# Fourier mixing with a routed expert layer: batch 0's A ahead of the constants in the store queue, selection and expert steps cut into single VectorE pieces, two bits a round for four batches

## The chip, the cores and the metric

The kernel runs on one core of a Trainium2 chip. The metric is the device time of one execution in microseconds; less is better. TensorE (PE), its weight loads (PEld), VectorE (DVE), ScalarE (ACT) and GpSimd (POOL) each take their instructions in order from a queue of their own, and SyncE (SP) issues nearly all transfers, in order too.

## The reference

Per batch (8 batches, 3136 rows, 256 columns) a real Fourier transform over the rows, a complex 256 by 256 product with bias and a soft threshold, the inverse transform, and then an expert layer for the 128 rows with the highest score.

```python
X = np.fft.rfft(x, axis=1)
Yr = Xr @ w_r - Xi @ w_i + b_r
Yi = Xr @ w_i + Xi @ w_r + b_i
Yr = np.sign(Yr) * np.maximum(np.abs(Yr) - lam, 0.0)   # Yi alike
y = np.fft.irfft(Y, n=x.shape[1], axis=1)
...
scores = np.einsum('bsd,d->bs', x, w_gate)             # x is y here
top_idx = np.argpartition(-scores[b], capacity)[:capacity]
h = np.maximum(xe @ w1, 0.0)
out[b, top_idx] = x[b, top_idx] + g[:, None] * (h @ w2)   # g: sigmoid of the score
```

## The kernel before

The 3136 rows are 98 by 32, so a transform is two short ones. The steps of a batch, with their names in the code and in the profile:
- s1, 8 tiles: x (tile `xt`, in the first batch also `cin`) is added and subtracted in halves (`xu`, `xv`, by GpSimd, in batch 0 by VectorE and GpSimd), multiplied by `first` into `s`, evicted by ScalarE into `at` and stored to DRAM as `As`.
- s2, 6 groups: `av` is loaded from `As`, once all 8 tiles of the batch are stored, multiplied by `second` into `px`, and split into a high and a low part (`Xh`, `Xl`).
- spectral, 6 groups: 24 products with `wh` and `wl` into `py`, then bias and threshold into `Y` (two halves: one by VectorE and ScalarE, the other by VectorE, ScalarE and GpSimd).
- s2i, 6 groups: `Y` times `second` into `s`, evicted into `ct`, stored as `Cs`; VectorE takes the scores' parts from the same banks (`junk`, `Csc`).
- s1i, 8 tiles: `cin` is loaded from `Cs` once the batch is stored, added and subtracted (`cu`, `cv`), multiplied into `s`, evicted into `ot` and stored as `out`.
- selection: the threshold of the 128 best rows is found bit by bit. In each round VectorE compares the scores with trial values (`c`), counts (`n`), PE adds the counts over the partitions (`n,tm` into `px`), and VectorE sets the bits (`ok`, `px`, `w`). With three bits a round 7 trial values are counted at once, and there are 12 rounds. Batches are selected in the groups 0-1, 2-3, 4-5, 6 and 7, one after the other. From the threshold come a mask, row numbers (`hot`, `row`) and `idxs`.
- expert layer, 8 times: GpSimd gathers `xe` by `idxs`; PE transposes it, multiplies by `w1s` and, in three products, by `w2h` and `w2l`; GpSimd scatters `ye` into `out`.

No order is written out by hand. While the program is built, a planner keeps an estimate of when each engine and each tile is free (in `Engine.given`, `mm` and `ld`, with `WIRE` as the queue's rate), and at each step takes the candidate with the lowest cost: waiting time plus its distance from its place in the sequence of 48 spectral steps (`F1` and `I1` place s1 and s1i, `LEAD` and `LAG` s2 and s2i). Loads, stores, sums and late steps are "sides": generators that go on when the planner's clock has come to them. The order so found is what each engine's queue holds; nothing is reordered at run time. After the last spectral step (`spec["t"] >= T`) only s1i, selection and experts are left.

The profile's lines for PE are nearly all L272 (`mm`), for VectorE, ScalarE and GpSimd L220 (the recording helper), for SyncE L301 (`ld`), so tiles' names tell the steps apart.

## Time and profile before

| | |
|---|---|
| median of 3 runs | 751.42 us (751.36 to 752.93) |
| the profiled execution | 746.76 us |
| its span, first to last instruction | 745.0 us |
| mean granted TensorE clock | 0.941 of full speed |
| PE busy | 673.3 us (90%) |
| VectorE, ScalarE, GpSimd busy | 407.5, 361.0, 394.8 us |
| bytes moved | 162.54 MB, mean 218 GB/s |

The engines' times overlap and don't add up to the span. A PE that is called busy isn't always at its full rate, since matmuls are pipelined and their ends are modelled; the row of the granted clock says when it ran slower (0.5 is 1.2 GHz, 1.0 is 2.4 GHz). "GB/s" is what all 16 DMA engines moved, "DMA share" how busy they were on average.

### The profile page before, as it was taken

How to read it: one execution, taken by the hardware profiler on the slowest of the kernel's cores; microseconds unless marked ns; L12 is line 12 of the kernel's file. 1: busy time of each engine (PE TensorE's matmuls, PEld its weight loads, DVE VectorE, ACT ScalarE, POOL GpSimd, SP SyncE). 2: the span in 40 equal slices, each digit the busy share in tenths (PEclk: the TensorE clock that was granted, in tenths of full speed). 3: DMA queues.
4: the chain of work that ended last, by engine and by line, in shares of the span. 5: the costliest groups of instructions: out<-in, count | busy, mean ns of one | idle time of the engine just before them, and what ended most of it. 6: DMA issues, size and time to landing. Idle time of an engine off the chain costs nothing.

```text
span 745.0 us, 19254 instructions
## 1 busy us (share of the span) xinstructions
PE 673.3 (90%) x7608; PEld 426.9 (57%) x7608; DVE 407.5 (55%) x1248; ACT 361.0 (48%) x766; POOL 394.8 (53%) x329
## 2 busy tenths in 40 slices
PE   4359999999999999999999999999989798699895
PEld 1127666666655565665555656665656465248784
DVE  6204455445358756453587664645876477546661
ACT  2324656566656655646556556465635234341110
POOL 5363636675776657747675577374540534362211
PEclk9569999999999999999999999999999899579997
DMA  8895878999798869887988798879845843781000
GB/s 249 280 287 186 257 229 254 223 279 303 233 295 266 287 194 273 263 277 234 277 278 286 211 272 276 280 209 279 247 136 130 214 110 114 173 240 59 29 15 22
DMA packets 85110, 162.54 MB, mean 218 GB/s; under 512 B 6334, under 2 KB 58907, under 8 KB 85019
## 3 DMA queue, kind: packets, MB, share of 16 engines
q1 hardware_dynamic: 83962, 159.13, 71.4%
q0 software_dynamic: 1056, 2.17, 0.9%
q8 instruction: 60, 0.98, 0.6%
q14 instruction: 32, 0.25, 0.1%
HBM read 83.23 MB, written 78.12 MB: 217 GB/s over the span
## 4 chain that ended last, share of the span: by engine, by line
PE 54%; DVE 9%; DMA 8%; issue 5%; POOL 2%; ACT 2%; SPq 0%; POOLq 0%; DVEq 0%; ACTq 0%
PE py L272 31%; PE s L272 17%; PE px L272 6%; DMA Cs<-ct 2%; DMA xt<-in_x 1%; DMA cin<-Ct 1%; DMA As<-at 1%; DVE c L220 1%; DVE px L220 1%; DVE hot L220 1%; DVE junk L220 1%; DMA cin<-Cs 1%; DVE n L220 1%; DVE py L220 1%; POOL xv L220 1%
## 5 line engine op out<-in xcount | busy, mean ns | idle before, releaser
L272 PE MATMUL py<-wh,Xh 128*128 128x512 f32 x384 | 170.5, 444 | 3.0 <-DVE YT L220 2.6
L272 PE MATMUL py<-wl,Xh 128*128 128x512 f32 x384 | 152.8, 398 | 0.0
L272 PE MATMUL py<-wh,Xl 128*128 128x512 f32 x384 | 152.7, 398 | 0.0
L220 POOL TENSOR_TENSOR cu<-cin 113x512 f32<-113x512 f32 x64 | 83.6, 1308 | 126.2 <-PE s L272 87.5
L220 DVE TENSOR_TENSOR Xl<-px,Xh 128x512 fp32r<-128x512 f32 x96 | 61.9, 686 | 132.4 <-ACT Xh L220 132.4
L220 POOL TENSOR_TENSOR xu<-xt 113x512 f32<-113x512 f32 x56 | 71.8, 1282 | 89.1 <-PE s L272 88.9
L272 PEld LDWEIGHTS py<-wh,Xh 128*128 128x128 f32 x384 | 73.1, 190 | 78.0 <-issue 53.4
L272 PE MATMUL s<-xu,first 49*64 49x512 f32 (+1 forms) x256 | 84.4, 661 | 22.3 <-ACT at L220 11.4
L220 ACT COPY ot<-s 113x512 f32<-113x512 f32 x128 | 68.7, 592 | 68.4 <-PE s L272 58.3
L220 ACT COPY at<-s 113x512 f32<-113x512 f32 x128 | 68.6, 588 | 58.9 <-PE s L272 43.2
L220 DVE CUSTOM_DVE_ANT_0 junk<-s,wgb 128x256 f32<-128x256 f32 x192 | 80.9, 421 | 26.3 <-ACT ct L220 12.9
L272 PE MATMUL s<-cu,first 49*64 49x512 f32 (+1 forms) x256 | 83.6, 658 | 7.1 <-POOL cu L220 5.7
L220 POOL TENSOR_TENSOR Y<-r,r 128x512 f32<-128x512 f32 x48 | 61.9, 1290 | 41.4 <-ACT r L220 19.3
L272 PEld LDWEIGHTS py<-wl,Xh 128*128 128x128 f32 x384 | 73.4, 191 | 17.1
L220 POOL TENSOR_TENSOR xv<-xt 113x512 f32<-113x512 f32 x60 | 78.2, 1305 | 8.9 <-DVE xt L220 4.7
L272 PE MATMUL s<-xv,first 49*64 49x512 f32 (+1 forms) x256 | 81.5, 662 | 0.2 <-POOL xv L220 0.2
L272 PE MATMUL s<-cv,first 64*64 64x512 f32 (+1 forms) x256 | 81.6, 661 | 0.0
L272 PEld LDWEIGHTS py<-wh,Xl 128*128 128x128 f32 x384 | 73.7, 192 | 9.5
L272 PEld LDWEIGHTS px<-second,av 64*64 64x64 f32 x3072 | 54.9, 138 | 37.4 <-issue 14.5
L220 ACT COPY ct<-s 128x256 f32<-128x256 f32 x192 | 57.6, 387 | 37.7 <-PE s L272 37.2
L220 POOL TENSOR_TENSOR cv<-cin 113x512 f32<-113x512 f32 x59 | 75.8, 1285 | 0.0
L272 PE MATMUL s<-Y,second 32*64 32x256 f32 x1536 | 65.4, 397 | 6.4 <-ACT ot L220 2.9
(128 smaller groups left out, 951.3 us busy)
## 6 DMA issues: line engine op xcount, KB each, us to landing
As<-at SPq DMA_DIRECT2D x64, 392.0 KB
out<-ot SPq DMA_DIRECT2D x64, 392.0 KB
av<-As SPq DMA_DIRECT2D x48, 512.0 KB
Cs<-ct SPq DMA_DIRECT2D x48, 512.0 KB
cin<-Cs SPq DMA_DIRECT2D x64, 384.0 KB
xt<-in_x SPq DMA_DIRECT2D x60, 392.0 KB
cin<-in_x SPq DMA_DIRECT2D x4, 392.0 KB
second<-t_second SPq DMA_DIRECT2D x2, 768.0 KB
```

Of the source, the lines that this page charges most:

```text
L220: return f(*args, **kw)
L272: return nc.tensor.matmul(out, a, b, start=start, stop=stop)
```

## The change

Four things change. First, the order of the first transfers: the loads of the constants become sides that wait until so many stores of batch 0's A have been issued (`behind_a` with the numbers in `CA`), and batch 0's odd tiles of A use the ring `ot`, which is idle then. Second, the VectorE parts of a selection round (`counts`, `digest`) and the steps of the expert layer (`copies`, `halves`, the final sum) are no longer issued together with their PE part: each is a side, issued when the planner finds VectorE free for it, in selection with a further delay (`LOWA`, `DB`). Third, the first two groups, four batches, take two bits a round: 3 trial values and 17 rounds. Fourth, the planner's numbers change, so the order of all engines changes in places.

```diff
-    WIRE = 370e3
+    WIRE = 300e3
...
     class Side:
-        def __init__(self, g):
-            self.g, self.over, self.need = g, False, None
+        def __init__(self, g, low=None):
...
-                    if w is None or w > t:
+                    if w is None or w > t - (s.low() if s.low else 0.0):
                         break
                     s.step()
                     again = True
+                    if s.low:
+                        break
                 if s.over:
                     sides.remove(s)
...
 
+    def behind_a(n):
+        return lambda: free["SP"] if stored.get(("A", 0), 0) + len(fed) >= n else None
+
+    def consts_s():
+        yield "SP", behind_a(CA[0])
+        ld(sec[0].rearrange("p j s -> p (j s)"), t_second[:, :NJ * 64])
+        yield "SP", behind_a(CA[3])
+        ld(tail, t_tail)
+        yield "SP", behind_a(CA[4])
+        ld(wgb, wg.rearrange("(o e) -> o e", o=1).broadcast_to([128, D]))
+        ld(sec[1].rearrange("p j s -> p (j s)"), t_second[:, NJ * 64:])
+
     def consts_w():
...
         ts = []
         for src in (w_r, w_i):
             ts.append(new(pool, [128, 2, D], F32, "r1", 2))
...
     def consts_bias():
+        vec.memset(m2l, -2.0 * LAM)
+        yield "SP", behind_a(CA[2])
         for c, src in enumerate((b_r, b_i)):
             row = src.rearrange("(o e) -> o e", o=1)
             ld(bias[:, c, :], row.broadcast_to([128, D]))
             ld(bias_t[33 * c:33 + 31 * c], row.broadcast_to([33 - 2 * c, D]))
-        vec.memset(m2l, -2.0 * LAM)
         yield "DVE", [bias, bias_t]
...
+        def counts(f, m):
             c = new(pool, [N1, nb, m, N2], BF16, "c_6" if nb == 1 else "c" + tag, 1)
...
+            yield "DVE", []
...
+        def digest(tot, m, i, nxt):
+            yield "DVE", [tot]
...
+            if nxt is None:
+                yield "DVE", []
...
+            m2, i2 = nxt
+            f = f[:, :, :m2]
+            vec.tensor_tensor(out=f, in0=digits[:, 8 * i2:8 * i2 + m2].rearrange("p (o m) -> p o m", o=1).broadcast_to([N1, nb, m2]),
+                              in1=wp.broadcast_to([N1, nb, m2]), op=ALU.bitwise_xor)
+            yield "DVE", []
+            yield from counts(f, m2)
...
+        rounds = [(2 ** (hi - i) - 1, i) for hi, i in zip([32] + cuts, cuts)]
+        side(first_keys(rounds[0][0]), low)
+        for (m, i), nxt in zip(rounds, rounds[1:] + [None]):
+            yield lambda: avail([st["n"]]) if st["n"] is not None else None
+            name = m_name()
+            tot = m_tile([N1, 4, nb, 2 ** bits - 1])
+            mm(tot[:, 0, :, :m], ones, st["n"])
+            st["n"] = None
+            hold(tot, name, side(digest(tot, m, i, nxt), low))
...
+        def copies():
+            yield "DVE", [px]
+            vec.tensor_copy(xT, px)
...
+            def halves(q, ph):
+                yield "ACT", [ph]
+                act.activation(out=hs[q][0], in_=ph, func=AF.Relu)
+                yield "DVE", [ph, hs[q][0]]
+                vec.scalar_tensor_tensor(out=hs[q][1], in0=ph, scalar=0.0, in1=hs[q][0].bitcast(F32), op0=ALU.max, op1=ALU.subtract)
+                st["h", q] = True
...
+            yield "DVE", [py, ga]
+            ye = new(pool, [n, D], F32, "ye", 1)
+            vec.scalar_tensor_tensor(out=ye, in0=py, scalar=ga, in1=xe, op0=ALU.mult, op1=ALU.add)
...
-        t = new(pool, [PT, 4, D], F32, "at", 3)
+        home = "ot" if b == 0 and i % 2 else "at"
+        t = new(pool, [PT, 4, D], F32, home, 3)
         tv = t.rearrange("p (r c) d -> p r (c d)", r=2)
...
+                fed.add((b, g))
...
-    EARLY, AHEAD, SW = 0.3,1.1,0
-    BACK, TAIL = 99,44
-    LAST = 2
-    PF = (0,0.1)
-    BEGIN, RATE, DB = 2.5,1.6,1
+    EARLY, AHEAD, SW = 0,1.1,0.2
+    BACK, TAIL = 99,40
+    LAST = 3
+    PF = (0,0.3)
+    BEGIN, RATE, DB = 2.5,2.2,0.3
+    LOWA = 0.4
     AHEADT, FA, TD = 0.7,2,0.5
     BE, BU, BY = 99, 99, 1.0
-    DG, GAP = 0.5,2
-    STEP, THW, FIL = 5,4,(8,2)
-    END = 0.1
-    GROUPS = ((0, 2), 3), ((2, 4), 3), ((4, 6), 3), ((6, 7), 3), ((7, 8), 3)
-    F1, I1 = [-1, 0, 0, 1, 2, 2, 3, 3],[9, 10, 10, 11, 12, 12, 13, 14]
-    LEAD, LAG = 0.95,2.06
+    DG, GAP = 0.5,0.5
+    STEP, THW, FIL = 5,4,(8,3)
+    END = 0.3
+    GROUPS = ((0, 2), 2), ((2, 4), 2), ((4, 6), 3), ((6, 7), 3), ((7, 8), 3)
+    F1, I1 = [-1, 0, 0, 1, 2, 2, 3, 3],[10, 10, 11, 12, 12, 13, 14, 15]
+    LEAD, LAG = 1.1,2.06
     NQ = 1
+    CA = 1,2,8,9,10,9
...
-        yield from select(bs, bits)
+        yield from select(bs, bits, lambda: 0.0 if spec["t"] >= T and bs.stop == B else LOWA - DB * owner[10 * bs.start - 200].behind())
...
+        side(a_side())
+        side(consts_s())
+        side(consts_w())
         side(consts_bias())
-        ld(sec[0].rearrange("p j s -> p (j s)"), t_second[:, :NJ * 64])
-        side(consts_w())
-        ld(tail, t_tail)
-        ld(wgb, wg.rearrange("(o e) -> o e", o=1).broadcast_to([128, D]))
-        side(a_side())
-        ld(sec[1].rearrange("p j s -> p (j s)"), t_second[:, NJ * 64:])
```

The order of SyncE's queue at the start, behind the table `first` and the first x tiles: `As` is the store of batch 0's A, `bias`, `second`, `r` (the two weights), `tail` and `wgb` are constants. Before:

```order
L301 DMA cin_94<-in_x 98x1024 x2
L301 DMA bias<-in_b_r 128x256
L301 DMA bias_t<-in_b_r 33x256
L301 DMA bias<-in_b_i 128x256
L301 DMA bias_t<-in_b_i 31x256
L301 DMA second_67<-t_second 128x1536
L301 DMA r_118<-in_w_r 128x2x256
L301 DMA r_120<-in_w_i 128x2x256
L301 DMA tail<-t_tail 64x161
L301 DMA wgb<-in_moe_w_gate 128x256
L301 DMA second_68<-t_second 128x1536
L301 DMA As<-at 98x1024
```

and in the changed kernel:

```order
L301 DMA cin_94<-in_x 98x1024 x2
L301 DMA As<-at 98x1024
L301 DMA second_67<-t_second 128x1536
L301 DMA As<-ot 98x1024
L301 DMA r_160<-in_w_r 128x2x256
L301 DMA r_162<-in_w_i 128x2x256
L301 DMA As<-at 98x1024
L301 DMA As<-ot 98x1024
L301 DMA As<-at 98x1024
L301 DMA As<-ot 98x1024
L301 DMA As<-at 98x1024
L301 DMA As<-ot 98x1024
```

The stores stood behind all constants and now stand between them; bias, `tail`, `wgb` and the second half of `second` come after the eighth store.

GpSimd's queue around the first `cin` of batch 6 (`cu` and `cv` are its sums, `Y` the last step of a half of a spectral group of batch 7). Before:

```order
L220 TENSOR_TENSOR Y<-r_7628,r_7532 128x512
L220 TENSOR_TENSOR cu<-cin_93 113x512
L220 TENSOR_TENSOR cv<-cin_93 113x512
L220 TENSOR_TENSOR cu<-cin_93 113x512
L220 TENSOR_TENSOR cv<-cin_93 113x512
L220 TENSOR_TENSOR Y<-r_7783,r_7677 128x512
L220 TENSOR_TENSOR cu<-cin_94 113x512
L220 TENSOR_TENSOR cv<-cin_94 113x512
L220 TENSOR_TENSOR Y<-r_7850,r_7832 128x512
```

and in the changed kernel:

```order
L220 TENSOR_TENSOR Y<-r_7750,r_7646 128x512
L220 TENSOR_TENSOR cu<-cin_93 113x512
L220 TENSOR_TENSOR cv<-cin_93 113x512
L220 TENSOR_TENSOR Y<-r_7855,r_7792 128x512
L220 TENSOR_TENSOR cu<-cin_93 113x512
L220 TENSOR_TENSOR cv<-cin_93 113x512
L220 TENSOR_TENSOR Y<-r_7979,r_7956 128x512
L220 TENSOR_TENSOR cu<-cin_94 113x512
L220 TENSOR_TENSOR cv<-cin_94 113x512
```

Two pairs of sums stood ahead of the second Y here; now one pair does.

PE's queue at the last selection (`row,hot` makes the row numbers of batch 7; `ident,xe` is the transpose of the rows gathered by them, `xT,w1s` an expert's first layer, `w2h` and `w2l` its second). Before:

```order
L272 MATMUL py<-w2h,hh 128x256
L272 MATMUL py<-w2h,hl 128x256
L272 MATMUL py<-w2l,hh 128x256
L272 MATMUL px_9367<-row,hot 128x34 x2
L285 MATMUL py<-ident,xe 128x128 x2
L272 MATMUL py<-xT,w1s 128x128 x16
L272 MATMUL py<-w2h,hh 128x256
```

and in the changed kernel, where 24 products of the second layer follow and then the transpose:

```order
L272 LDWEIGHTS tm
L272 MATMUL px_9432<-cnt,tm 98x1
L272 MATMUL py<-xT,w1s 128x128 x8
L272 MATMUL px_9455<-row,hot 128x34 x2
L272 MATMUL py<-xT,w1s 128x128 x8
L272 MATMUL py<-w2h,hh 128x256
L272 MATMUL py<-w2h,hl 128x256
L272 MATMUL py<-w2l,hh 128x256
```

The last gather had no PE work behind `row,hot`; now half of a first layer and a whole second layer of batch 6's experts stand there.

## Rows read from the trace of the kernel before

**Rows 1.** The page, parts 1 and 2: busy time, granted clock in 40 slices.

```profile
PE 673.3 (90%) x7608; PEld 426.9 (57%) x7608; DVE 407.5 (55%) x1248; ACT 361.0 (48%) x766; POOL 394.8 (53%) x329
...
PEclk9569999999999999999999999999999899579997
```

**Rows 2.** Stretches on all engines: busy us (instructions), clock, DMA share, GB/s.

```profile
0.00:50.00 50.00, 21.76 (x88) 5.96 (x88) 16.31 (x20) 15.18 (x27) 28.87 (x29) 0.79 0.85 270
50.00:56.00 6.00, 4.44 (x129) 3.95 (x129) 1.29 (x2) 1.21 (x3) 0.42 (x4) 0.50 1.01 293
...
238.00:388.00 150.00, 146.68 (x1781) 88.57 (x1774) 87.69 (x272) 85.23 (x182) 96.97 (x79) 1.00 0.86 259
388.00:534.50 146.50, 145.00 (x1783) 87.84 (x1774) 87.68 (x272) 85.00 (x183) 89.87 (x73) 1.00 0.86 257
```

**Rows 3.** Timeline of ScalarE at the start: start us, us, instruction, idle before.

```profile
13.85 1.07 ACT L220 COPY at<-s 113x512 f32<-113x512 f32 x2 [0.63 <-PE s L272]
15.67 1.07 ACT L220 COPY at<-s 113x512 f32<-113x512 f32 x2 [0.75 <-PE s L272]
26.77 1.07 ACT L220 COPY at<-s 113x512 f32<-113x512 f32 x2 [10.03 <-DMA As<-at]
```

**Rows 4.** Timeline of the queue of SyncE, merged: start us, us, issues.

```profile
23.43 12.05 SPq L301 DMA_DIRECT2D As<-at  x4
...
43.28 1.01 SPq L301 DMA_DIRECT2D av<-As  x2
...
93.93 0.94 SPq L301 DMA_DIRECT2D av<-As  x2
```

**Rows 5.** Timeline of PE at the start.

```profile
50.04 1.99 PE L272 MATMUL px<-second,av 64*64 64x64 f32 x64 [6.66 <-DMA av<-As]
53.42 2.57 PE L272 MATMUL px<-second,av 64*64 64x64 f32 x64 [1.40 <-DVE Xl L220]
55.92 0.79 PE L272 MATMUL py<-wh,Xh 128*128 128x512 f32 x1
```

**Rows 6.** The chain that ended last: start us, us, what (one A load).

```profile
298.22 10.19 DMA As<-at
308.49 4.27 DMA av<-As
```

**Rows 7.** Timeline of PE at the first s2 of batch 1.

```profile
101.49 1.16 PE L272 MATMUL px<-second,av 64*64 64x64 f32 x64 [1.12 <-DMA av<-As]
```

**Rows 8.** Groups by shape, whole span: count, busy us, mean ns, idle before.

```profile
L220 DVE TENSOR_TENSOR c<-scores,px 98x448 bf16<-98x448 f32 x30 | 18.6, 621 | 1.0
L220 DVE TENSOR_REDUCE n<-c 98x14 bf16<-98x448 bf16 x30 | 18.6, 620 | 1.0
...
L220 DVE TENSOR_TENSOR c<-scores,px 98x224 bf16<-98x224 f32 x20 | 7.7, 387 | 0.7
...
L272 PE MATMUL px<-n,tm 98*98 98x14 bf16 x30 | 5.1, 172 | 0.6 <-DVE Xl L220 0.2 <-DVE n L220 0.2
```

**Rows 9.** Timeline of PE in batch 7.

```profile
586.81 1.13 PE L272 MATMUL s<-Y,second 32*64 32x256 f32 x4 [2.90 <-ACT ot L220]
```

**Rows 10.** Timeline of ScalarE in batch 7.

```profile
584.90 0.72 ACT L220 ACTIVATE r<-r,m2l 128x512 f32<-128x512 f32 x1 [6.04 <-POOL Y L220]
```

**Rows 11.** Timeline of GpSimd in batch 7.

```profile
578.66 1.30 POOL L220 TENSOR_TENSOR cu<-cin 113x512 f32<-113x512 f32 x1 [9.05 <-DMA cin<-Ct]
...
583.59 1.27 POOL L220 TENSOR_TENSOR Y<-r,r 128x512 f32<-128x512 f32 x1
```

**Rows 12.** Timeline of PE at the end.

```profile
715.80 2.12 PE L272 MATMUL py<-xT,w1s 128*128 128x128 f32 x17
...
722.20 0.36 PE L272 MATMUL py<-w2h,hh 128*128 128x256 f32 x1
...
725.14 0.53 PE L272 MATMUL px<-row,hot 98*128 98x34 f32 x4
...
730.19 0.69 PE L285 MATMUL py<-ident,xe 128*128 128x128 f32 x2 [4.51 <-DMA xe<-out,idxs]
```

More of the change, by code (lines that the diff above doesn't have):

```diff
@@ L347, in fourier_moe @@
     class Side:
-        def __init__(self, g):
-            self.g, self.over, self.need = g, False, None
+        def __init__(self, g, low=None):
+            self.g, self.over, self.need, self.low = g, False, None, low
             self.step()
@@ L363, in fourier_moe, with side @@
     sides = []
-    def side(g):
-        s = Side(g)
+    def side(g, low=None):
+        s = Side(g, low)
         if not s.over:
@@ L497, in m_tile, with select @@
         return new(ps, shape, F32, name, 1)
-    def select(bs, bits):
+    def select(bs, bits, lag):
         nb = bs.stop - bs.start
@@ L506, in select @@
             cuts.append(max(cuts[-1] - bits, 0))
-        w = wp = None
-        for hi, i in zip([32] + cuts, cuts):
-            m = 2 ** (hi - i) - 1
-            if w is None:
-                f = new(pool, [N1, nb, m], U32, "f" + tag, 1)
-                vec.memset(f, 0)
-            else:
-                f = small[:, 3, :, :m]
-                vec.tensor_tensor(out=f, in0=digits[:, 8 * i:8 * i + m].rearrange("p (o m) -> p o m", o=1).broadcast_to([N1, nb, m]),
-                                  in1=wp.broadcast_to([N1, nb, m]), op=ALU.bitwise_xor)
+        st = {"n": None, "w": None, "small": None, "wp": None}
+        low = lag
+        def counts(f, m):
             c = new(pool, [N1, nb, m, N2], BF16, "c_6" if nb == 1 else "c" + tag, 1)
@@ L640, in hidden, with combine @@
             hs.append([t[:, 4 * q:4 * q + 4, :n] for t in both] if spare else pair([128, 4, n], "h", 2))
-            act.activation(out=hs[q][0], in_=ph, func=AF.Relu)
-            vec.scalar_tensor_tensor(out=hs[q][1], in0=ph, scalar=0.0, in1=hs[q][0].bitcast(F32), op0=ALU.max, op1=ALU.subtract)
-            yield [xT] if q + 1 < FF // 512 else list(hs[q])
-    def combine(b, k, idx, xe, ga, hs):
+            st["h", q] = False
+            def halves(q, ph):
[4 more added lines that the diff above has]
+                st["h", q] = True
+            hold(ph, name, side(halves(q, ph)))
+            if q + 1 < FF // 512:
+                yield [xT]
+            else:
+                yield lambda: avail([t for h in hs for t in h]) if all(st["h", z] for z in range(FF // 512)) else None
+    def combine(b, k, idx, xe, ga, hs, st):
         n = min(128, cap - 128 * k)
+        drain(st["gate"])
+        name = e_name()
         py = e_tile([n, D])
@@ L650, in combine @@
             mm3(py, hh, hl, w2h[:, f, :], w2l[:, f, :], f == 0, f == FF // 128 - 1)
-        ye = new(pool, [n, D], F32, "ye", 1)
-        vec.scalar_tensor_tensor(out=ye, in0=py, scalar=ga, in1=xe, op0=ALU.mult, op1=ALU.add)
         def put():
+            yield "DVE", [py, ga]
+            ye = new(pool, [n, D], F32, "ye", 1)
+            vec.scalar_tensor_tensor(out=ye, in0=py, scalar=ga, in1=xe, op0=ALU.mult, op1=ALU.add)
+            hold(ye, "ye", box[0])
             yield "POOL", [ye]
@@ L726, in put @@
             stored["A", b] = stored.get(("A", b), 0) + 1
-        hold(t, "at", side(put()))
+        hold(t, home, side(put()))
     def a_side():
@@ L995, in when @@
             if self.rank < 0 and spec["t"] < T:
-                t = max(t, free["DVE"] - DG - DB * self.behind(), turned_at[0] + GAP)
+                t = max(t, free["DVE"] - DG - DB * self.behind(), turned_at[0] + GAP) if DG < 9 else t
             elif s2m["t"] < T and TD:
@@ L1003, in spawn @@
         t.stop = stop
+        if stop is not None:
+            owner[rank] = t
         if not t.over:
@@ L1047, in ffn @@
             turns[0] += 1
-            xT, ga = prepare(*it, spare)
-            yield [xT]
+            st = {"xT": False}
+            xT, ga = prepare(*it, spare, st)
+            yield lambda: avail([xT]) if st["xT"] else None
             hs = []
-            yield from hidden(*it[:2], xT, hs, spare)
-            combine(*it, ga, hs)
+            yield from hidden(*it[:2], xT, hs, spare, st)
+            combine(*it, ga, hs, st)
             ffns[0] += 1
```

72 lines of the change are left out of this document (46 added, 26 removed).

## Prediction

> **What bounds the kernel now.** I read the page first, then the stretches, then the waits at the two ends. The page says that TensorE is busy for 673.3 of 745.0 us, and the row of its granted clock shows two places below full: slices 2 to 4, and the last quarter [rows 1]. The table of stretches explains why they differ. From 238 to 388 us, two whole batches, PE is busy for 146.7 of 150 us at clock 1.00; from 388 to 534.5 it is the same [rows 2]. There only PE work counts, and I look for no large gain. The DMA share there is 0.86 at 259 GB/s, so the queue has some room, not much. In the first 50 us PE is busy for 21.8 us only, while the queue carries 270 GB/s at a share of 0.85 [rows 2]: the start is bound by the queue and by what stands in it. So three places can give time: the start, the last batch or so, and single stalls between them.
>
> **The start.** Today's stores of batch 0's A are late. ScalarE evicts two tiles 1.82 us apart (13.85 and 15.67), then stands still for 10.03 us, to 26.77, because the ring `at` has three buffers and the first store has not landed [rows 3]. The store queue itself shows the end of it: four stores take 12.05 us to issue from 23.43, and the first load of `av` can be issued only at 43.28, when all eight stores are in [rows 4]. Its data let PE begin s2 at 50.04; the first spectral product runs at 55.92 [rows 5].
>
> In the new order of the queue (shown above) the stores come right behind the x loads, with only the first table and the two weights between. I add the shapes in order of issue: the eighth store ends at 11.2 MB now and at 7.46 MB then. At the 270 GB/s of this stretch, and 2 us for the first bytes, 7.46 MB are through at about 30 us, 31 with the completion. The tiles are there in time: eight evictions at 1.82 us end near 26, and six buffers instead of three let the seventh wait for a store that is the first in the queue. The load of `av` takes 4.27 us from issue to landing where it was last on the chain [rows 6], so s2 starts near 35.5. Between s2 and the first spectral product the new PE order has one s1 of batch 1, whose x stands just behind `av`: 0.4 MB more, two additions on GpSimd, some 2 us of products at the low clock. I put the first spectral product at 41.5: 14.4 us earlier.
>
> Not all of it stays. Three s1 that ran in idle time ahead of s2 now run behind it: 3 x 0.9 = 2.7 us of PE, so PE alone keeps 11.7. And the queue must bring batch 1's A sooner. Its last store stands at 23.3 MB in either order, its first load was issued at 93.93 [rows 4], and PE waited 1.12 us for it until 101.49 [rows 7]. From 35.3 us and 8.7 MB on, 14.6 MB are left; at 293 GB/s, the rate at a share of 1.01 [rows 2], that is 50 us: 85.5, 8.4 earlier. At 270 it is 54 us: 89.3, 4.6 earlier. Of the wait that ends today on the load some is slack, so I take **-9.5**, between the queue's 8.4 and PE's 11.7; bounds -4.6 and -11.7. After that the bytes from batch to batch are the same or fewer, and PE sets the pace, so I expect the shift to be kept.
>
> The Trainium skill, "DMA: Bandwidth & Descriptors", section "Where 436 GB/s comes from", puts the limit of HBM to SBUF traffic for one core at about 358 GB/s. The stretch with a share of 1.01 moved 293 GB/s, so this trace does not bear that out for this mix of loads and stores; by the page's figure the queue would never bind, and the term would be -11.7.
>
> **Two bits a round.** Two groups of two batches go from 12 rounds to 17. On VectorE a full round compares and counts 448 elements, 621 and 620 ns; 224 elements take 387 [rows 8], so 192 come to 354. The five small operations per round stay, so per group VectorE does about 2 us more in all, in pieces half as long. It is busy for less than 60% of 238 to 388 [rows 2], which hides it. On PE ten more rounds cost ten products of 0.17 us [rows 8]: **+1.7**; lower bound 0, where they fall into a gap. If the cover goes, the price is the wait of the slower rival below. The smaller pieces may also take VectorE's block of 1.2 us from ahead of the copies that PE waits for; PE's idle time from 238 to 388 is 3.3 us, so a gain is bounded by about 3 per two batches, and I take 0.
>
> **Y behind a late load.** In batch 7 PE stands from 583.9 to 586.81 in the middle of s2i, for ScalarE [rows 9]. ScalarE had waited 6.04 us, to 584.90, for GpSimd's Y [rows 10]. GpSimd had waited 9.05 us for the first `cin` of batch 6 and then did two pairs of sums before that Y, which started at 583.59 [rows 11]. The new GpSimd order has one pair ahead of it: two sums of some 1.25 us less, **-2.5**. Bounds: 0, if the load lands later by as much, and -6 if the Y then runs before anything waits.
>
> **The end.** After the last selection's products PE waits 4.51 us for the gathered rows, to 730.19 [rows 12]; nothing else is left to do. In the new order half of one expert's first layer and its whole second layer stand in that gap: 16 products, of which 17 took 2.12 us, and 24 like those from 722.20 to 725.14, 2.94 us; together 4.9 us [rows 12]. This work is taken from ahead of the selection, so the gap is filled: **-4.5**. Bounds: 0, if the selection's chain and not PE decides when its last round ends; -6 with the shorter way to the gather.
>
> **Sum.** -9.5 + 1.7 - 2.5 - 4.5 = -14.8 us. The profiled execution took 746.76 us, which would become 732; it is 4.66 us under the median of the runs, so on the median of 751.42 the forecast is **736.6**. Other moved orders (s1i one step later, s2 and s2i next to each other) keep PE's number of mode changes within two of 283, and I price them at nothing; PE's idle time in the middle covers some of it, and if it does not, a step of s1i more in the end costs its 0.9 us.
>
> **Rivals.**
> *The queue takes it back.* The lead-in's loads are only reordered, so if the queue gives 270 GB/s behind `av`, as it did on average to 50 us [rows 2], the start keeps 4.6, and if the end's chain is the selection, nothing is won there: -4.6 + 1.7 = -2.9, 748.5. For it: that mean; against: the 293 at a share of 1.01.
> *The queue never binds.* Then the start keeps 11.7, the Y comes in time (-6) and the end saves 4.5 to 6: -11.7 + 1.7 - 6 - 5 = -21, 730. For it: the stretch at 293; against: the mean of 259 over the busiest 150 us [rows 2]. The page's limit cited above would speak for it.
> *Slower: PE waits at every round.* Each round's pieces are now placed singly between other VectorE work, and PE takes its products in order. Behind a round's product in PE's queue stand the spectral products, and everything waits for those. If each of the 70 rounds held PE for one reduction of 0.35 us, that is 24.5 us and +9.7 in all: 761. It decides from 14.8/70 = 0.21 us a round. Against it: in the new order six or more spectral products stand between most rounds, 1.4 us and more, beside copies.
> *Nothing.* The stores move, but s2 waits for something else in the start (the bias, x of batch 1), and the end's filler only moves its gap: within 1.5 us of before.
>
> **How the numbers follow.** A change under 0.2% (1.5 us) can't be told from none here. Forecast 0.50 (its own range 731 to 742), queue takes it back 0.20, queue never binds 0.20, slower 0.07, nothing 0.03. Range 723 to 749: from below the faster rival's 730, with its two bounds added, to the first rival's end. Faster 0.89, same 0.04, slower 0.07; the first rival is split 0.19 to 0.01.
>
> **What would show it.** The first `av` issue near 31, the first spectral product near 41 and no wait of ScalarE for the stores of A; the first `av` of batch 1 issued at 84 to 89. If that is at 93, the queue rival holds. From one batch's first s2 to the next but one still about 150 us. One pair of sums between the first `cin` of batch 6 and the next Y. No wait over 1 us for the last gather. I am wrong if PE's idle time in the middle grows by more than 3 us per two batches, or if the tail from batch 7's last spectral product to the end is no shorter than now.

## The result, and the profile after

The changed kernel takes 710.84 us (median of 4 runs, 708.59 to 712.16), the kernel before 751.39 us in the runs beside them: a ratio of 0.947 (0.942 to 0.952), 40.6 us or 5.3% faster. That is outside the range forecast (723 to 749). The profiled execution took 712.16 us with a span of 710.4 us, against 746.76 and 745.0 before. So of the 40.6 us the two traces show 34.6; the rest is that before's profiled execution lies below its median and the other above.

A table of places makes the comparison. It holds the start of the first spectral product of a step, read from PE's rows (six steps a batch, so step 12 begins batch 2), and "last" is the last spectral product of all.

| | before | after | gained in this stretch |
|---|---|---|---|
| step 0 | 55.92 | 45.16 | 10.8 |
| step 12 | 179.41 | 170.63 | -2.0 (start in all: **8.8**) |
| step 42 | 549.74 | 532.52 | **8.4** |
| step 44 | 574.17 | 558.96 | -2.0 |
| step 46 | 604.28 | 579.84 | **9.2** |
| last | 627.19 | 600.09 | 2.7 |
| end | 744.96 | 710.37 | **7.5** |

The middle gains in batches 2 and 3 alone: steps 12 to 24 take 141.4 us instead of 151.0, steps 24 to 36 take 150.6 instead of 147.0, steps 36 to 42 take 69.9 instead of 72.3. A second trace of the changed kernel has 363.9 us between steps 12 and 42 where this one has 361.9, so a difference of some 2 us between two traces tells nothing.

The page of the changed kernel, parts 1 and 2 (busy time; granted clock in 40 slices of 17.8 us), which answers to [rows 1]:

```profile
PE 656.2 (92%) x7618; PEld 417.9 (59%) x7618; DVE 417.5 (59%) x1322; ACT 360.9 (51%) x766; POOL 393.5 (55%) x325
...
PEclk9769999999999999998999999999999999589999
```

PE is busy 17 us less with ten products more, and the row of the clock has two slices below 9 in the last quarter, where before it had four. The stretches of the changed kernel (columns as in [rows 2]: PE, PEld, VectorE, ScalarE, GpSimd; the second from step 12 to step 42, the third to the last spectral product, the fourth to the end):

```profile
0.00:50.00 50.00, 23.40 (x214) 8.81 (x214) 19.08 (x23) 14.77 (x27) 22.22 (x19) 0.80 0.89 260
170.63:532.52 361.89, 357.09 (x4425) 219.19 (x4421) 224.84 (x742) 213.78 (x455) 235.67 (x189) 0.99 0.90 264
532.52:600.09 67.57, 63.60 (x743) 42.47 (x741) 48.71 (x172) 31.53 (x70) 25.23 (x21) 0.97 0.62 163
600.09:710.37 110.28, 93.44 (x673) 69.52 (x671) 66.60 (x234) 29.56 (x65) 34.71 (x29) 0.88 0.36 104
```

and the same last three of the kernel before:

```profile
179.41:549.74 370.33, 364.39 (x4479) 220.42 (x4473) 219.50 (x674) 213.99 (x456) 235.30 (x189) 1.00 0.85 257
549.74:627.19 77.45, 69.79 (x714) 45.06 (x708) 48.21 (x157) 33.12 (x75) 27.18 (x22) 0.91 0.55 145
627.19:744.96 117.77, 91.77 (x635) 70.55 (x633) 63.53 (x243) 26.33 (x57) 32.14 (x28) 0.81 0.33 91
```

Read idle time as length minus the first busy number. In the middle it hardly changes (from 5.9 to 4.8 us), yet the stretch is 8.4 us shorter: PE's *busy* time fell. In the last two it falls from 7.7 to 4.0 and from 26.0 to 16.8 us, and the clock is higher in both.

**The start went as forecast.** SyncE's queue after (the first and last store of batch 0's A, the first `av`, the first `av` of batch 1), to be held against [rows 4]:

```profile
13.25 0.32 SPq L301 DMA_DIRECT2D As<-at  x1
...
24.72 0.31 SPq L301 DMA_DIRECT2D As<-ot  x1
...
29.78 0.39 SPq L301 DMA_DIRECT2D av<-As  x1
...
87.29 0.93 SPq L301 DMA_DIRECT2D av<-As  x2
```

and PE there, to be held against [rows 5]:

```profile
38.44 1.99 PE L272 MATMUL px<-second,av 64*64 64x64 f32 x64 [14.89 <-DMA av<-As]
42.04 1.96 PE L272 MATMUL s<-xu,first 64*64 64x512 f32 x2 [1.61 <-POOL xu L220]
...
45.16 0.79 PE L272 MATMUL py<-wh,Xh 128*128 128x512 f32 x1
```

The load is issued at 29.78 (forecast 31) and batch 1's first at 87.29 (forecast 84 to 89). Between them one thing is worse: s2 begins 8.66 us after the issue, not 4.27, and the s1 of batch 1 then waits 1.61 us for its sums, so the first spectral product stands at 45.16, not 41.5.

**The wait for Y is gone.** GpSimd after, around the first `cin` of batch 6 (compare [rows 11]):

```profile
562.61 1.29 POOL L220 TENSOR_TENSOR cu<-cin 113x512 f32<-113x512 f32 x1 [9.48 <-DMA cin<-Ct]
563.84 1.30 POOL L220 TENSOR_TENSOR cv<-cin 113x512 f32<-113x512 f32 x1
565.09 1.29 POOL L220 TENSOR_TENSOR Y<-r,r 128x512 f32<-128x512 f32 x1
```

The load is as late as before (GpSimd stands 9.48 us), but one pair of sums stands ahead of Y, and PE does not wait. What it had cost shows in two stretches of the kernel before, 8 us each, from the wait on:

```profile
581.70:589.70 8.00, 3.59 (x82) 2.00 (x84) 2.54 (x8) 3.29 (x6) 6.84 (x6) 0.93 1.06 276
589.70:597.70 8.00, 8.00 (x45) 5.38 (x38) 2.83 (x14) 1.56 (x8) 0.00 (x0) 0.50 0.39 128
```

and in the same place of the changed kernel:

```profile
558.00:574.00 16.00, 15.89 (x187) 11.22 (x188) 10.71 (x42) 8.44 (x22) 7.49 (x6) 1.00 1.04 239
```

Before, PE stood still for 4.4 of 8 us, and in the next 8 us it was busy all the time at a clock of 0.50, the 1.2 GHz level: so some 4 us of work were lost behind a wait of 4.4 (an estimate: half of the 8 us). After, 16 us without a gap and at full clock.

**The end has fewer waits.** Groups of PE from the last spectral product to the end, before:

```profile
L272 PE MATMUL s<-cu,first 64*64 64x512 f32 (+1 forms) x44 | 19.6, 884 | 5.7 <-POOL cu L220 5.7
...
L285 PE MATMUL py<-ident,xe 128*128 128x128 f32 x16 | 3.9, 332 | 6.3 <-DMA xe<-out,idxs 4.5 <-DVE ye L220 1.8
L272 PE MATMUL px<-n,tm 98*98 98x7 bf16 (+1 forms) x21 | 3.9, 184 | 6.1 <-DVE n L220 6.1
```

and after:

```profile
L272 PE MATMUL s<-cu,first 64*64 64x512 f32 (+1 forms) x48 | 20.2, 806 | 1.5 <-DVE cu L220 1.5
...
L272 PE MATMUL px<-n,tm 98*98 98x7 bf16 (+1 forms) x19 | 3.6, 187 | 2.7 <-DVE n L220 2.6
L285 PE MATMUL py<-ident,xe 128*128 128x128 f32 x16 | 3.5, 322 | 0.0
```

The last number ahead of the arrow is the idle time before the group. The wait for gathered rows is gone (6.3 to 0.0, of which 4.5 us was the last gather), s1i's fell from 5.7 to 1.5, and the rounds' from 6.1 to 2.7. The experts' work left in the stretch is the same; one step of s2i (32 products, some 3 us) and one tile of s1i more stand in it, and new waits came up, the longest for `Csc` (1.9 us) and for the mask (1.8).

### The profile page after: what moved, and what is told of

Read it like the earlier page. It is cut to its first block, busy times and chain, and to the rows that moved or that the text cites. A ratio compares the mean times of both kernels' runs of the same rounds, so it can differ in the third digit from the quotient of the medians.

```text
span 710.4 us, 19358 instructions
## 1 busy us (share of the span) xinstructions
PE 656.2 (92%) x7618; PEld 417.9 (59%) x7618; DVE 417.5 (59%) x1322; ACT 360.9 (51%) x766; POOL 393.5 (55%) x325
## 5 line engine op out<-in xcount | busy, mean ns | idle before, releaser
L220 POOL TENSOR_TENSOR cu<-cin 113x512 f32<-113x512 f32 x56 | 72.2, 1290 | 102.5 <-PE s L272 89.2
L220 ACT COPY ot<-s 113x512 f32<-113x512 f32 x136 | 72.9, 594 | 64.4 <-PE s L272 58.0
L220 POOL TENSOR_TENSOR cv<-cin 113x512 f32<-113x512 f32 x64 | 85.0, 1331 | 12.0 <-DMA cin<-Ct 7.6
L220 ACT COPY at<-s 113x512 f32<-113x512 f32 x120 | 64.4, 592 | 48.4 <-PE s L272 38.9
L272 PE MATMUL s<-xu,first 64*64 64x512 f32 (+1 forms) x256 | 76.3, 639 | 11.7 <-DVE xu L220 10.1
L272 PEld LDWEIGHTS py<-wl,Xh 128*128 128x128 f32 x384 | 72.8, 190 | 16.8
L272 PE MATMUL s<-cu,first 49*64 49x512 f32 (+1 forms) x256 | 77.9, 651 | 1.5 <-DVE cu L220 1.5
L272 PEld LDWEIGHTS px<-second,av 64*64 64x64 f32 x3072 | 53.3, 138 | 43.7 <-DMA av<-As 18.0
L272 PE MATMUL px<-second,av 64*64 64x64 f32 x3072 | 59.0, 224 | 20.5 <-DMA av<-As 16.7
L272 PE MATMUL s<-cv,first 49*64 49x512 f32 (+1 forms) x256 | 76.6, 653 | 0.0
L272 PE MATMUL s<-xv,first 64*64 64x512 f32 (+1 forms) x256 | 71.9, 639 | 0.0
```

What stands on the lines that cost most here:

```text
L220: return f(*args, **kw)
L272: return nc.tensor.matmul(out, a, b, start=start, stop=stop)
```

## The experiments

Each ratio is to the kernel before, run beside it on the same chip. The kernels before differ by some us between chips (medians of 744.3 to 751.4), so variants run on different chips are compared by ratio. Steps and stretches are read from one trace of each variant. A short name of the changed kernel's parts: the *lead* (order of the first transfers, ring `ot`), the *pieces* (VectorE's parts as sides), *two bits*, and the *numbers* (the planner's).

### One part taken back

The old lead in the changed kernel:

```diff
-        home = "ot" if b == 0 and i % 2 else "at"
+        home = "at"
...
+        ld(sec[0].rearrange("p j s -> p (j s)"), t_second[:, :NJ * 64])
+        side(consts_w())
```

> The changed kernel with the first transfers in the old order: constants ahead of batch 0's A, three buffers for A. Theory start (the new order of the queue gives what the trace shows at batch 1's first spectral step, about 10 us, and it is kept to the end): 719 to 723 us. Rival (later waits give it back, so the whole gain comes from the rest): 709 to 713 us.

724.13 us, 0.970 (0.962 to 0.978), just above the 719 to 723 of its theory. Step 0 begins at 60.77, step 12 at 183.11, which is 12.5 later than in the changed kernel. The start is worth some 12 us here.

VectorE's (and ScalarE's) parts issued at once, the numbers new:

```diff
-            hold(tot, name, side(digest(tot, m, i, nxt), low))
+            at_once(digest(tot, m, i, nxt))
```

> The changed kernel with the VectorE and ScalarE parts of selection rounds and experts issued at once with their PE part, as before; lead, planner's numbers and two bits stay. Theory pieces (the gain behind the start, about 25 to 30 us, comes from the pieces): 730 to 740 us. Rival numbers (it comes from the planner's numbers, which place s1, s1i, s2 and s2i): 708 to 716 us.

725.38 us, 0.972 (0.965 to 0.980), between theory and rival. It loses in batch 6: steps 36 to 42 take 79.25 us (69.92 in the changed kernel). Steps 44 to 46 keep their 21 us, so the wait for Y is gone without the pieces too.

All planner's numbers old that the kernel before has too, with lead, pieces and two bits:

```diff
-    BEGIN, RATE, DB = 2.5,2.2,0.3
+    BEGIN, RATE, DB = 2.5,1.6,1
...
-    LEAD, LAG = 1.1,2.06
+    LEAD, LAG = 0.95,2.06
```

> The changed kernel with the planner's numbers of before (queue rate, EARLY, SW, TAIL, LAST, PF, RATE, DB, GAP, FIL, END, places of s1i, LEAD); lead, pieces and two bits stay. Theory numbers: 730 to 740 us. Rival pieces: 708 to 716 us. In between, both are needed.

741.26 us, 0.992 (0.988 to 0.996), just above the theory's range: without the numbers, all the rest together gives under 1%. Steps 12 to 42 take 376.0 us, more than before the change.

Three bits for all groups:

```diff
-    GROUPS = ((0, 2), 2), ((2, 4), 2), ((4, 6), 3), ((6, 7), 3), ((7, 8), 3)
+    GROUPS = ((0, 2), 3), ((2, 4), 3), ((4, 6), 3), ((6, 7), 3), ((7, 8), 3)
```

> The changed kernel with three bits a round in all groups. By the prediction's term ten rounds less are worth 1.7 us: 708 to 710 us. Rival (blocks of VectorE half as long spare PE waits): 713 to 718 us.

709.41 us, 0.949 (0.942 to 0.956): the same as the changed kernel (0.947). Two bits are worth nothing that these runs can tell; the forecast's +1.7 is allowed by them.

### One part alone

The new lead in the kernel before:

```diff
-        t = new(pool, [PT, 4, D], F32, "at", 3)
+        home = "ot" if b == 0 and i % 2 else "at"
+        t = new(pool, [PT, 4, D], F32, home, 3)
...
+    CA = 1,2,8,9,10,9
```

> The kernel before with the new order of the first transfers alone (constants behind the stores of batch 0's A, the second ring for its odd tiles); planner's numbers, rounds and experts as before. If the start is worth by itself what it is worth in the changed kernel (13 us): 732 to 738 us beside 747. Rival (the old numbers don't keep it): 742 to 748. The wait of Y in batch 7 is unchanged if the numbers or the pieces took it away, and gone if any shift of the order does.

739.38 us, 0.991 (0.987 to 0.995), between theory and rival, and as much as lead, pieces and two bits give together with the old numbers (0.992). Step 12 begins at 171.98, 7.4 us sooner than before, and step 42 is still 7.6 us ahead; 4.5 remain at the end. Steps 44 to 46 take 30.45 us: the wait for Y stays.

The new numbers in the kernel before:

```diff
-    BEGIN, RATE, DB = 2.5,1.6,1
+    BEGIN, RATE, DB = 2.5,2.2,0.3
...
-    LEAD, LAG = 0.95,2.06
+    LEAD, LAG = 1.1,2.06
```

> The kernel before with the planner's new numbers alone. Theory numbers (they carry the gain behind the start by themselves): 728 to 738 us beside 747. Rival (they suit only a kernel with the new lead or with pieces): 742 us or more.

742.6 us, 0.997 (0.994 to 1.000): next to nothing, as its rival said. Steps 44 to 46 take 20.27 us, so the numbers alone remove the wait for Y, and lose it again: batch 6 takes 79.88 us.

### Which of the numbers

The old places:

```diff
-    EARLY, AHEAD, SW = 0,1.1,0.2
+    EARLY, AHEAD, SW = 0,1.1,0
...
-    F1, I1 = [-1, 0, 0, 1, 2, 2, 3, 3],[10, 10, 11, 12, 12, 13, 14, 15]
-    LEAD, LAG = 1.1,2.06
+    F1, I1 = [-1, 0, 0, 1, 2, 2, 3, 3],[9, 10, 10, 11, 12, 12, 13, 14]
+    LEAD, LAG = 0.95,2.06
```

> The changed kernel with SW at 0 and the old LEAD and places of s1i: s1i one step earlier, s2 later, no cost for a change of PE's mode. If these make the middle shorter (8 us from batch 2 to batch 6): 716 to 722 us, with batches 2 and 3 at 148 us and more instead of 141.4. Rival: 708 to 714.

731.3 us, 0.981 (0.976 to 0.987): some 20 us of the 40, more than theory and rival had. The next four split it.

SW alone back to 0:

```diff
-    EARLY, AHEAD, SW = 0,1.1,0.2
+    EARLY, AHEAD, SW = 0,1.1,0
```

> The changed kernel with SW at 0, as before: a change of the kind of work on PE costs the planner nothing; nothing is left out. The old places (SW, LEAD, I1 together) cost 20 us. Theory: SW does most of it, because it decides how many products of one kind follow each other: 722 to 731, with steps 12 to 36 some 6 us longer. Rival: LEAD and I1 do it, since they put s2 further ahead of its spectral step and s1i a step later: 709 to 715 here.

711.71 us, 0.953 (0.944 to 0.961): nothing. The theory that put most of it on SW fell.

LEAD and I1 back, SW new:

```diff
-    F1, I1 = [-1, 0, 0, 1, 2, 2, 3, 3],[10, 10, 11, 12, 12, 13, 14, 15]
-    LEAD, LAG = 1.1,2.06
+    F1, I1 = [-1, 0, 0, 1, 2, 2, 3, 3],[9, 10, 10, 11, 12, 12, 13, 14]
+    LEAD, LAG = 0.95,2.06
```

> The changed kernel with the old LEAD (0.95 for 1.1) and the old I1 (s1i about one step sooner), SW at the new 0.2; nothing is left out. The other half of the old places. Theory (SW does most): 709 to 715. Rival (LEAD and I1 do it): 722 to 731, with the loss in steps 12 to 36, where s1i comes before its loads are in or s2 comes too late for the split on VectorE.

728.24 us, 0.977 (0.968 to 0.985): these two hold most of it, though not where the rival put the loss: steps 12 to 36 take 288.5 us, and the end takes 119.0.

LEAD alone back:

```diff
-    LEAD, LAG = 1.1,2.06
+    LEAD, LAG = 0.95,2.06
```

> The changed kernel with the old LEAD alone (0.95 for 1.1: s2 a little later before its spectral step); nothing is left out. LEAD and I1 together cost 17 us, of which about 9 behind the last spectral product, where PE stands for 22.0 instead of 10.1 us. Theory: I1 does that, since s1i a step sooner leaves less of it as filler for the last selections; LEAD alone: 709 to 716, the stretch from the last spectral product to the end 110 to 113. Rival: LEAD does it: 720 or more and 117 or more at the end.

717.51 us, 0.960 (0.953 to 0.967), 1.5 us above its theory, with the end at 110.7 us as in the changed kernel. It loses 4.5 us between steps 0 and 12, where PE's timeline shows one wait that the changed kernel hasn't:

```profile
144.94 2.36 PE L272 MATMUL s<-Y,second 32*64 32x256 f32 x28 [3.91 <-ACT at L220]
```

I1 alone back:

```diff
-    F1, I1 = [-1, 0, 0, 1, 2, 2, 3, 3],[10, 10, 11, 12, 12, 13, 14, 15]
+    F1, I1 = [-1, 0, 0, 1, 2, 2, 3, 3],[9, 10, 10, 11, 12, 12, 13, 14]
```

> The changed kernel with the old I1 alone (s1i about one step sooner); nothing is left out. Theory: it brings back most of the 17 us: 720 to 730, with 116 to 120 us from the last spectral product to the end and PE standing for 17 us or more there. Rival (LEAD does it, or only both together): 709 to 716.

724.74 us, 0.972 (0.964 to 0.979). From the last spectral product to the end it takes 119.4 us, not 110.3. PE's groups in that stretch:

```profile
L272 PE MATMUL s<-cu,first 64*64 64x512 f32 (+1 forms) x44 | 21.4, 833 | 5.1 <-DVE cu L220 4.3 <-DVE ok L220 0.8
...
L285 PE MATMUL py<-ident,xe 128*128 128x128 f32 x16 | 3.6, 308 | 4.6 <-DVE ye L220 1.8 <-DMA xe<-out,idxs 1.7 <-PE s L272 1.1
L272 PE MATMUL px<-n,tm 98*98 98x7 bf16 (+1 forms) x19 | 3.4, 180 | 5.6 <-DVE n L220 5.6
```

There are 88 products of s1i's two halves as before the change (44 in this row; 48 in the changed kernel's). One tile less of s1i is left as filler, and the three waits of the kernel before are back at 5.1, 4.6 and 5.6 us.

The old numbers of the late steps:

```diff
-    BACK, TAIL = 99,40
-    LAST = 3
-    PF = (0,0.3)
+    BACK, TAIL = 99,44
+    LAST = 2
+    PF = (0,0.1)
...
-    END = 0.3
+    END = 0.1
```

> The changed kernel with the old numbers for the late steps (TAIL 44, LAST 2, PF 0.1, FIL (8, 2), END 0.1); nothing is left out. Theory: the 7.5 us that the end is shorter, and the wait for Y that is gone (9.2), come from pieces and selection, not from these numbers: 709 to 715, steps 44 to 46 in 20 to 22 us. Rival: these numbers place the last steps, and the old ones bring back the wait or the longer end: 718 to 728, with steps 44 to 46 at 26 us or more or 117 us from the last spectral product to the end.

719.19 us, 0.962 (0.953 to 0.971), inside the rival's range. The end takes 117.9 us, as the rival had it; steps 44 to 46 stay at 22.1, so the wait for Y does not come back.

The old rate of the queue:

```diff
-    WIRE = 300e3
+    WIRE = 370e3
...
-    EARLY, AHEAD, SW = 0,1.1,0.2
+    EARLY, AHEAD, SW = 0.3,1.1,0.2
```

> The changed kernel with the planner's old rate for the queue (WIRE 370e3) and the old EARLY (0.3), the last of the moved numbers that no run has taken back by itself; nothing is left out. Theory: with the old rate the planner takes loads for landed that are not, as where PE waited for the sums of a late load: 713 to 722. Rival: these numbers move little that PE waits for: 708 to 713.

721.78 us, 0.967 (0.963 to 0.971), 11 us more than the changed kernel beside it on the same chip (its run is below). Against the first trace of the changed kernel 4.7 of it stand in the first batch (steps 0 to 6) and 5.5 at the end.

### The pace of selection

The old pace:

```diff
-    BEGIN, RATE, DB = 2.5,2.2,0.3
+    BEGIN, RATE, DB = 2.5,1.6,1
...
-    DG, GAP = 0.5,0.5
+    DG, GAP = 0.5,2
```

> The changed kernel with the old numbers for selection rounds (RATE 1.6, DB 1, GAP 2). If it is rounds placed too late or too close that made the kernel with all old numbers slow (batch 6 and the end 20 us longer): 722 to 738 us. Rival: 708 to 714.

721.6 us, 0.970 (0.964 to 0.976). Here the two halves go against each other; the stretches from step 12 to 36 and from the last spectral product to the end:

```profile
167.36:449.62 282.26, 281.62 (x3565) 172.23 (x3561) 175.78 (x585) 170.11 (x361) 193.16 (x155) 1.00 0.93 274
...
594.13:719.15 125.02, 95.17 (x644) 72.20 (x643) 71.73 (x260) 27.10 (x59) 31.05 (x25) 0.81 0.30 88
```

It comes out just under its theory's range. The four batches take 9.7 us less than in the changed kernel (282.3 against 292.0), with 0.6 us of idle time on PE; the end takes 14.7 us more. That suggested a kernel with the old pace early and the new one late:

```diff
+        def early(self):
+            return self.rank < -170 and spec["t"] < 40
...
-                t = max(t, free["DVE"] - DG - DB * self.behind(), turned_at[0] + GAP) if DG < 9 else t
+                t = max(t, free["DVE"] - DG - (1.0 if self.early() else DB) * self.behind(), turned_at[0] + (2.0 if self.early() else GAP)) if DG < 9 else t
```

> The changed kernel with the old pace of selection (RATE 1.6, DB 1, GAP 2) for the first two groups until spectral step 40, and the new pace from there on; nothing is left out. Theory: the new pace costs about 11 us in the middle, because rounds of the first four batches stand among the spectral steps sooner and more densely (old selection numbers reached step 42 at 521.4 instead of 532.5), and it pays for that at the end, where 20 and not 24 rounds are left behind the last spectral step. With both, step 42 should begin at 519 to 526, the end from the last spectral product be about 110 as in the changed kernel, and the time be 698 to 705. Rival: what the middle gains with the old pace is work put off, and it comes back between step 42 and the end whatever the pace is there: step 42 early, but 118 us or more from the last spectral product, and 708 to 716.

712.06 us, 0.956 (0.947 to 0.965): no gain to be told. The time is the rival's, its reason is not: the end is even shorter than the theory had it (106.3 us). But steps 36 to 42 take 75.3 us, not 69.9; the third group was pushed together there, and PE waits in batch 6:

```profile
500.26 0.61 PE L272 MATMUL s<-cu,first 64*64 64x512 f32 x1 [2.05 <-ACT ot L220]
```

The same until step 33:

```diff
-            return self.rank < -170 and spec["t"] < 40
+            return self.rank < -170 and spec["t"] < 33
```

> As the kernel with the early groups at the old pace, but until spectral step 33 instead of 40, so that the second group ends at step 36 and the third begins at step 39 as in the changed kernel (nothing is left out). The kernel before it lost 5 us between steps 36 and 46, where its third group was squeezed. Theory: the old pace is worth its gain in steps 12 to 36 (451.6 instead of 462.6 us at step 36) wherever the next group isn't crowded: step 42 at 521 to 526, no wait over 3 us at about 497 us, and 698 to 706 in all. Rival: the rounds that the second group has to make up between steps 32 and 36 cost what the earlier steps gained: step 42 at 529 or later, and 707 to 714.

706.01 us, 0.946 (0.941 to 0.951), but the kernel before took 744.3 us on that chip, so this told little against the changed kernel's 0.947. Both were then run side by side, the changed kernel first:

> The changed kernel itself, unaltered, beside the next kernel on the same chip, since the runs of before differ by some us from one call to another. Theory (the old pace of selection in the early groups is worth about 4 to 5 us): this one 709 to 712, the next one 4 to 5 us less. Rival: the difference between the calls was the chip's: within 2 us of each other.

710.95 us, 0.952 (0.948 to 0.956): 36 us less than the kernel before, which is faster on this chip than on the first.

> The kernel with the old pace of selection for the first two groups until step 33, again, beside the changed kernel on the same chip; nothing is left out. Theory: 704 to 707 and 4 to 5 us less than the changed kernel. Rival: the same as the changed kernel within 2 us.

704.24 us, 0.943 (0.939 to 0.947): 6.7 us less than the changed kernel on the same chip, with step 36 at 451.78 and 107.4 us from the last spectral product to the end. The six runs of each do not overlap (702.2 to 707.7 and 709.4 to 712.8). This version beats both kernels.

## Why the prediction was wrong

The direction, the mechanism at the start, and the places at which the end and the Y would gain were right. Four terms of the sum were given as -9.5, +1.7, -2.5 and -4.5, and all else "at nothing": -14.8 us. The profiled executions differ by 34.6 us, 19.8 more. Of these, 10.1 are in the middle (8.4 gained where +1.7 was given), 6.7 in the stretch of the Y, 3.0 at the end; the start gave 0.7 less, and the other two stretches nearly cancel. Neither of the two signs of being wrong that the prediction named came up. But one sign of being right failed: two batches were still to take about 150 us, and batches 2 and 3 took 141.4.

**The start: right.** 8.8 us are left of it at step 12, inside the bounds; alone it gives 7.4, taken out of the changed kernel 12.5, which is beyond the bound of 11.7. Two steps of the path were off. The bytes end one store short: with the eighth store the shapes add to 7.86 MB, not 7.46, which is 1.5 us at 270 GB/s; the load of `av` was issued at 29.78 all the same. And from that issue to the first product took 8.66 us, twice the 4.27 of [rows 6]. The four loads of bias stand right ahead of it in the queue, issued from 25.08 to 28.50, and 214 GB/s moved while PE waited; which of the two made it late was not tried.

**Two bits: not refuted.** A term of 1.7 us is too small for these runs (0.949 against 0.947).

**Y behind a late load: mechanism right, size wrong.** The forecast took two sums of 1.25 us for the gain, with a bound of -6. The stretch from step 44 to 46 is 9.2 us shorter. Two things were missing: the wait was 4.4 us and not 2.9 (1.5 more for `Csc` stand behind it), and the clock, since behind the gap PE worked at 0.50 for 8 us. The Trainium skill, "TensorE: Matmul & The Clock Gate", section "HAM oscillation — how this bites in real kernels", says that waits between bursts of products make the clock drop and that the next burst then runs cold; the two 8 us stretches above agree, with 1.00 in the changed kernel in their place. Runs also show that the pair of sums was not tied to one part: the wait is gone with the new numbers alone (20.3 us), and with lead, pieces and old numbers (20.5), but not with the lead alone (30.5).

**The end: one of three waits priced.** The 4.5 us of the last gather went as forecast. The other two, s1i for GpSimd's sums and the rounds for VectorE's counts, gave 4.2 and 3.4 us more; they were not in the sum. New waits took back part of this, so that PE's idle time fell by 9.2 us. The old I1 alone brings all three back, and with it one tile of s1i less is left for that stretch; that this tile is what fills the waits is the likely reading, not tried apart. The prediction had seen in that later s1i a cost of 0.9 us at most; taken back, it loses 14. PE's busy time rose by 1.7 us at the same time, and 7.5 us net came out.

**The moved orders "at nothing": the step that failed most.** The prediction priced places and numbers at nothing because PE's idle time from 238 to 388 is 3.3 us, and took that as the bound for what smaller pieces or other places could give in two batches. Batches 2 and 3 gained 9.7 us, the middle in all 8.4, of which only 1.1 are idle time. The bound was wrong because waiting also hides inside PE's busy time. A tile of s1 or s1i has two halves of four products; when nothing holds them, they run beside each other and begin within 0.02 us:

```profile
270.02 0.64 PE L272 MATMUL s<-cv,first 64*64 64x512 f32 x1
270.02 0.64 PE L272 MATMUL s<-cu,first 49*64 49x512 f32 x1
```

The two halves write two banks of PE's output memory. One held s1 of the kernel before, PE's rows (the last product of its first half, the first of its second):

```profile
284.82 0.59 PE L272 MATMUL s<-xv,first 64*64 64x512 f32 x1
285.69 0.61 PE L272 MATMUL s<-xu,first 49*64 49x512 f32 x1 [0.28 <-DVE Csc L220]
```

and VectorE at that time:

```profile
283.19 0.62 DVE L220 TENSOR_TENSOR c<-scores,px 98x448 bf16<-98x448 f32 x1
283.84 0.62 DVE L220 TENSOR_REDUCE n<-c 98x14 bf16<-98x448 bf16 x1
284.51 0.69 DVE L220 TENSOR_TENSOR r<-py,bias 128x512 f32<-128x512 f32 x1
285.12 0.41 DVE L220 CUSTOM_DVE_ANT_0 junk<-s,wgb 128x256 f32<-128x256 f32 x1
285.46 0.08 DVE L220 DVE_READ_ACCUMULATOR2_ANT Csc<- 128x1 f32 x1
```

The second half of s1 needs the bank `s` that `junk` and `Csc` still have to read, and those stand behind a round's `c` and `n` and the `r` of a spectral step. Its first product starts 0.87 us after the last of the first half and 1.36 us after the first one; the row shows 0.28 us of idle time, since PE counts as busy while the first half runs alone, up to the modelled end of its last product, 0.59 us after its start. The whole s1 took 1.93 us instead of 0.91 to 1.02, and PE counted as busy for 1.65 of it. The Trainium skill, "Perfetto Trace Analysis", its opening note, calls matmul busy time a bad measure of how close a kernel is to its limit, because matmuls are pipelined; this row shows by how much it can mislead here.

The last of a tile's eight products starts 0.50 us after the first where nothing holds it. Between steps 12 and 42 it starts over 0.85 us after it in 18 of 79 tiles of the kernel before and in 6 of the changed one, two of which ran at a clock of 0.50 to 0.60. By the releasers that the profile infers, `Csc` on VectorE held a product in 11 of the 18, ScalarE's evictions in the other 7; in the changed kernel none was held by `Csc`. There a round lets the reads pass; VectorE:

```profile
270.58 0.17 DVE L220 TENSOR_TENSOR px<-digits,px 98x6 uint32<-98x6 uint32 x1
270.66 0.42 DVE L220 CUSTOM_DVE_ANT_0 junk<-s,wgb 128x256 f32<-128x256 f32 x1
271.00 0.08 DVE L220 DVE_READ_ACCUMULATOR2_ANT Csc<- 128x1 f32 x1
271.00 0.35 DVE L220 TENSOR_TENSOR c<-scores,px 98x192 bf16<-98x192 f32 x1
271.27 0.42 DVE L220 CUSTOM_DVE_ANT_0 junk<-s,wgb 128x256 f32<-128x256 f32 x1
```

PE's groups of s1 and s1i from step 12 to 42 give the size, before:

```profile
L272 PE MATMUL s<-cv,first 64*64 64x512 f32 (+1 forms) x164 | 49.8, 612 | 0.0
...
L272 PE MATMUL s<-xv,first 64*64 64x512 f32 (+1 forms) x152 | 46.7, 614 | 0.0
```

and after:

```profile
L272 PE MATMUL s<-cv,first 64*64 64x512 f32 (+1 forms) x164 | 45.8, 617 | 0.0
...
L272 PE MATMUL s<-xv,first 64*64 64x512 f32 (+1 forms) x154 | 42.4, 623 | 0.0
```

Each product takes as long as before (612 and 617 ns), but a group's busy time, in which products beside each other count once, is 4.0 and 4.3 us shorter, because the halves run beside each other more often: that is as much as the middle's 8.4 (s2i and s2 take 3.1 us less too, 1.3 of it because 70 products of s2 lie outside the stretch now; the rounds take 1.8 more, the spectral products 1.9).

Neither pieces nor numbers give the shorter middle alone. Steps 12 to 42 take:

| | old numbers | new numbers |
|---|---|---|
| parts at once | 370.3 (before) | 375.1 (before with the numbers), 367.7 (with lead and two bits too) |
| pieces, lead and two bits | 376.0 | 361.9 (after) |

The lead alone leaves the middle at 370.1, and three bits in the changed kernel leave it at 361.5, so neither the lead nor the two bits make the difference. The two slow kernels, pieces with old numbers and new numbers without pieces:

```profile
172.46:548.42 375.96, 362.05 (x4423) 219.25 (x4418) 227.91 (x720) 213.68 (x455) 235.16 (x189) 0.98 0.86 252
...
177.28:552.35 375.07, 360.99 (x4481) 221.48 (x4477) 231.76 (x694) 213.21 (x456) 235.94 (x189) 0.99 0.87 255
```

and PE's waits for a round's counts in the same two stretches (us in total, times, longest):

```profile
PE px L272 <- DVE n L220: 4.9, 3, 2.6
...
PE px L272 <- DVE n L220: 6.0, 4, 2.9
```

They lose by something else than the kernel before. PE's busy time fell in them as well, from 364.4 to 362.1 and 361.0 us, and 6 and 12 tiles are held instead of 18; but PE's idle time rose from 5.9 to 13.9 and 14.1 us, and the waits for counts are the largest single one. In this table only the pair has few held tiles and little idle time (4.8 us). That the numbers place steps for a VectorE that can be interrupted is a likely reason, not shown. Nor is each of the new numbers good for the middle: with the old pace of selection it is shorter still, 354.0.

**The rivals.** "The queue never binds" (730) came nearest, but its reasons give 21 us, and no single wait accounts for the rest. "PE waits at every round" is refuted for this kernel: the rounds show 0.1 us of idle time between steps 12 and 42. In the three mixed kernels of the table such waits did come: 6.0, 3.9 and 4.9 us in the same stretch. "Nothing" is refuted by the 40 us. "The queue takes it back" is refuted by the first `av` of batch 1 at 87.29.

**What stays open.** Which row of the order makes I1, WIRE and the late steps' numbers worth 8 to 14 us each by the medians is only partly traced: their losses overlap (one by one they add up to more than 40 us) and each new order moves all engines. That the wait of s1 at 284 us is due to the round ahead of `junk` is read from VectorE's order and from the releasers, not tried by itself: no run moves the reads of a bank ahead of a round and leaves all else.

## What to carry to other kernels

PE's idle time is no upper bound for what a better order gives: compare the time from one step's first product to the next with the same step's shortest, and look at what holds the bank of a group that takes twice as long. Look then at idle time too: a change that frees the banks can bring waits elsewhere, as the two slow kernels show. Price a wait of PE with the stretch at half clock behind it, which here cost as much as the wait. Where a change cuts work into pieces and re-tunes a planner's numbers at once, neither may be worth what the pair is (here 0.992 with the pieces and the lead, 0.997 with the numbers, 0.947 with all), so price the pair. And one pace need not serve the whole kernel: the old pace until step 33, where it does not yet crowd the next group, gives 704 us.

## What was not expected of the hardware

The clock also fell where PE's rows show little idle time. In the changed kernel PE waited 1.56 us for `Csc` at 603.90 and 0.34 more, between products of s2i; the stretches of 3 us there:

```profile
603.00:606.00 3.00, 1.76 (x5) 0.62 (x6) 2.16 (x12) 1.20 (x4) 0.96 (x1) 0.78 0.50 172
606.00:609.00 3.00, 3.00 (x31) 1.52 (x30) 1.13 (x5) 0.64 (x3) 0.00 (x0) 0.50 0.22 79
609.00:612.00 3.00, 3.00 (x12) 0.67 (x12) 1.77 (x9) 1.51 (x5) 0.00 (x0) 0.50 0.48 168
```

It stayed at 0.50 up to 621 us although PE counts as busy for nearly all of it. Here too busy time hides a part: from 602.34 to 606.2 us PE began five products of s2i, of which 32 take 1.12 us elsewhere (at 278.80 in the kernel before). So the idle time of a stretch alone does not tell how little PE did before its clock fell. The clock also showed 0.50 from 318 to 324 us, behind two waits of 1.11 us each (to 316.71 for `Xl` and to 320.08 for `YT`).
